# Loading v once per batch and bounding its norms with ScalarE's sums, in a hashed attention followed by an MoE block

## The chip, the cores and the metric

The kernel runs on one core of one Trainium2 chip. The metric is device time in microseconds (us), the median of several executions. Five engines run side by side, each with its own queue that is worked off in order: TensorE (PE in the profile, with its weight loads as PEld), VectorE (DVE), ScalarE (ACT), GpSimd (POOL) and SyncE (SP). SP computes nothing here and issues all DMA transfers.

## The reference, cut to what matters

```python
# batch 4, heads 8, sequence 768, head size 64; proj 64 x 6
q_bits = (einsum('bhsd,dk->bhsk', q, proj) > 0)      # the same for k
mask = q_bucket[:, :, :, None] == k_bucket[:, :, None, :]
scores = where(mask, scale * q @ k.T, -1e9)
e = exp(scores - max(scores)); attn = e / (sum(e) + 1e-9)
x = (attn @ v)  # brought to 3072 tokens x 512
h = maximum(x @ w_in, 0)                              # 512 -> 2048
out = (h * h) @ w_out                                 # 2048 -> 512
```

## The kernel before

**Precision.** The large products run in 16-bit floats, in high and low parts: a float32 value is multiplied by a power of two, rounded to f16 (the high part, `move`), and the remainder is rounded again (the low part, `left`, always one VectorE instruction when the scale is a tile). The power of two must come from a bound on the data, so each batch's v is read through once for a norm before it is split. That norm is only an upper bound: it sets an exponent.

**Tiling.** A *unit* (`unit`) is 128 query rows of one head: the scores (tile `pS`) on PE, their maximum `nmx` on DVE, `e` = exp on ACT with its row sum `sm`, the reciprocal `rv`, the high part of `hl` mostly on ACT and the low part on DVE, and a transposing DMA from `hl` to `aT`. There are 192 units. A *visit* is three units of each of two heads and ends with `av`, the product of `aT` with the split values `VV` (PE, tile `pA`, result `xx`). Eight visits make a batch. After four visits of one half of a batch, one of eight MoE stages (`moe`) follows: 16 steps `f`, each 12 matmuls into `pm`, the square on ACT, high and low parts `g`, and 9 matmuls into `po`. The weights `win` and `wo` are loaded and split while the first batch runs. At the end of the first MoE stage `align` multiplies all 16 blocks of `wo` by a power of two.

**The values.** `values(b, hp)` gives the split values of a pair of heads, [128, 2, 6, 128] f16, 3072 bytes per partition. The first call for a batch runs `scale_values`: for each of the four pairs of heads it loads v (384 KB, tile `RV`, two buffers), squares it in place, reduces the squares on DVE to 12 sums `rows` and these to one maximum `vtop`, and then forms the bound over all partitions with a small matmul (`top`, `dg`, `pt`, `norm`). Afterwards `values` loads the same 384 KB again into an `RV`, since the squares have overwritten it, and splits that into `VV` (four buffers).

**What sets the order.** The kernel records all operations first. `Program.order` is a planner: it walks the operations with a priority from their `rank` and with its own cost figures, and it chooses the engine where several may do an operation (`move`, `square`). It keeps the best of several rounds, and every engine's queue is then written out in that order (`emit`). Where the planner sees a gap on PE before the first `pm`, `emit` writes filler matmuls (`idle<-ones`) into it. So a change to one operation can move many others on all engines.

The lines to follow: `square`, `scales` and `load` are helpers within the main function; `scale_values` and `values` are called from the loop over visits with the rank `u - 6 + PREP`, plus `VALUES`.

Of the kernel before, what the change touches and what calls it, by code (L numbers as in the profile page):

```python
# [23 lines left out]
P = 128  # L24
# [3 lines left out]
KC = S // P  # L28
# [5 lines left out]
ASC = float(2.0**14)  # L34


BUFS = dict(xx=12, hl=3, raw=2, f=7, e=3, aT=3, g=2, A=2, Q=2, L=2, M=2, RV=2, VV=4)
PRICE = dict(pe=1, dve=3.57, act=0.3, pool=3.06, sp=0.43)
AHEAD, DELAY, LAG = 60, 2500, 1.0

ROUNDS, BEHIND = 4, 40000

PREP, STACKS, VALUES = -9, 0, 2
WIN_RANK, WOUT_RANK = (18, 2.0), (30, 2.5)
# [17 lines left out]
        ("act", "dve"): 100, ("act", "pool"): 180, ("pool", "dve"): 70, ("pool", "act"): 50, ("pool", "sp"): 140}  # L62


SWITCH = 95


class Buffer:
# [44 lines left out]
class Program:  # L113
# [59 lines left out]
    @staticmethod  # L173
    def cost(key, name, args, kw):

        size = lambda x: int(np.prod(x.shape[1:]))
        column = {F32: 4 / 2.4, F32R: 0.445}
        if name == "matmuls":

            side = {32: 4, 64: 2}.get(size(args[0][0][1]), 1)  # L180
            t = sum(size(a[2]) * column.get(a[2].dtype, 1 / 2.4) + 7 for a, _ in args) / side
            return t, t
        kinds = [x.rec.kind if isinstance(x, View) else "" for x in args]
        ptr = any(isinstance(x, View) and x.shape[-1] == 1 for x in args[2:3])
        n = max(size(args[0]), size(args[1]) if isinstance(args[1], View) else 0)
        if key == "pe":
            t = max(107, size(args[2]) * column.get(args[2].dtype, 1 / 2.4) + 3)
            return t, t
        if name.startswith("dma"):
            b = int(np.prod(args[0].shape)) * mybir.dt.size(args[0].dtype)  # L190
            inside = name == "dma_start_transpose" or kinds[:2] == ["sb", "sb"]
            busy = 1040 if key == "pool" else (650 if inside else 475) + 50 * (key == "act")
            return busy, b / (175 if name == "dma_start_transpose" else 314)
        if key == "act":
            t = 93 * (isinstance(kw.get("scale"), View) + isinstance(kw.get("bias"), View)) + (51 if "psum" in kinds[:2] else 93) + n / 1.2 + 93 * ("accum_out" in kw)
        elif key == "pool":
            t = 147 + n * (2.1 if args[0].dtype == F32 or args[0].dtype == F32R else 1.88) if name == "tensor_tensor" else 161 + n / 1.2 + 83 * ptr
        else:
            fast = name in ("tensor_copy", "tensor_scalar") and "psum" not in kinds[:2]
            both = len(args) > 3 and isinstance(args[3], View) and args[3].shape[-1] == 1  # L200
            t = 67 + n / (1.92 if fast else 0.96) + 62 * (ptr and (fast or name == "scalar_tensor_tensor")) + 100 * both
        return t, t

    @staticmethod
    def tiling(o):

        _, w, x = (o.args[0][0] if o.name == "matmuls" else o.args)[:3]
        size = lambda n: min(m for m in (32, 64, 128) if n <= m)
        return size(w.shape[0]), 128 if w.dtype == F32R else size(int(np.prod(w.shape[1:])))

    @staticmethod
    def port(key, name, args, kw):
# [82 lines left out]
    def forward(self, prio, near):  # L295
        ops = self.ops
        left = [len(o.deps) + len(o.after) for o in ops]
        for o in ops:
            o.queue, o.open = None, set()
        keys = ("pe", "dve", "act", "pool", "sp")  # L300
        later = {k: [] for k in keys}
        ready = {k: [] for k in keys}
        free = dict.fromkeys(keys, 0.0)
        out, dma, dge, held, kind = [], 0.0, 0.0, 0.0, None

        def offer(i):
            for w in ops[i].ways:
                k = w[0].key
                at = max([ops[j].end + LAG * LAGS.get((ops[j].queue.key, k), 200) for j in ops[i].deps] + [ops[j].start for j in ops[i].after], default=0.0)
                heapq.heappush(later[k], (at, i))  # L310
                ops[i].open.add(k)

        for i in range(len(ops)):
            if not left[i]:
                offer(i)
        while True:
            best = None
            for k in keys:
                if ready[k]:
                    t = free[k]  # L320
                elif later[k]:
                    t = max(free[k], later[k][0][0])
                else:
                    continue
                if best is None or t < best[0]:
                    best = t, k
            if best is None:
                break
            t, k = best
            while later[k] and later[k][0][0] <= t:  # L330
                i = heapq.heappop(later[k])[1]
                heapq.heappush(ready[k], (prio[i], i))
            i = heapq.heappop(ready[k])[1]
            o = ops[i]
            if o.queue is not None:
                continue
            way = next(w for w in o.ways if w[0].key == k)
            if way[5] and held > t and (ready[k] or later[k] and later[k][0][0] < held):
                heapq.heappush(later[k], (held, i))
                continue  # L340
            ends = {}
            if len(o.ways) > 1:
                for w in o.ways:
                    k2 = w[0].key
                    ahead = sum(ops[j].ways[0][4][0] / len(ops[j].open) for r, j in ready[k2] if ops[j].queue is None and r <= prio[i] + near and j != i)
                    ends[k2] = max(free[k2], t, held if w[5] else 0.0) + w[4][0] * PRICE[k2] + ahead + DELAY * w[1].startswith("dma")
            if any(e < ends[k] and k2 in o.open for k2, e in ends.items()):
                o.open.discard(k)
                continue
            o.queue, o.name, o.args, o.kw, (busy, done), port = way  # L350
            if port:
                t = max(t, held)
                held = t + busy
            if k == "pe":
                last, kind = kind, self.tiling(o)
                if last != kind:
                    busy, done = busy + SWITCH, done + SWITCH
            o.start, o.busy = t, busy
            if o.name.startswith("dma"):
                dge = max(dge, t) + busy if k != "pool" else dge  # L360
                busy = dge - t if k != "pool" else busy
                dma = max(dma, t + busy + (650 if k != "pool" else 450))
                if o.name == "dma_start_transpose":
                    o.busy = busy = dma + 467 - t
                dma += done
                done = dma + 910 - t
            free[k], o.end = t + busy, t + done
            out.append(i)
            for j in o.users:
                left[j] -= 1  # L370
                if not left[j]:
                    offer(j)
        assert len(out) == len(ops), (len(out), len(ops))
        return out
# [40 lines left out]
def lsh_attention_moe(ctx: ExitStack, tc, kq, v, proj2, w_in, w_out, consts, out):  # L415
# [27 lines left out]
    def sb(shape, dtype, name, bufs=1, tag=None):  # L443
        return pr.tile(sbp, "sb", shape, dtype, name, BUFS.get(tag or name, bufs), tag)
# [164 lines left out]
                out.append(((Q, A), (M, L)))  # L609
        return out  # L610

    vscales = {}

    def load(b, hp):
        RV = sb([P, 2, KC, D], F32, "RV")
        send(RV, v[b, hp])
        return RV

    def scale_values(b):

        tops = sb([P, H // 2], F32, "vtop", 2)
        for hp in range(H // 2):
            RV = load(b, hp)
            rows = sb([P, 2 * KC], F32, "rows", 2)
            square(RV, RV)
            dve.tensor_reduce(rows, RV.rearrange("p h c d -> p (h c) d"), AX.X, ALU.add)
            dve.tensor_reduce(tops[:, hp : hp + 1], rows, AX.X, ALU.max)
        top = sb([P, 1], F32, "top")
        dve.tensor_reduce(top, tops, AX.X, ALU.max)
        dg = sb([P, P], BF16, "dg")  # L630
        move(dg, ident, top)
        pt = ps([P, 512], F32, "pt", tag="misc")[:, 0:P]
        pe.matmul(pt, ones, dg, start=True, stop=True)
        norm = sb([P, 1], F32, "norm")
        dve.tensor_reduce(norm, pt, AX.X, ALU.max)
        vscales[b] = scales(norm, "v", 4)

    def values(b, hp):

        r0 = pr.rank  # L640
        pr.rank = r0 + VALUES
        if b not in vscales:
            scale_values(b)
        RV = load(b, hp)
        VV = sb([P, 2, KC, 2 * D], F16, "VV")
        move(VV[:, :, :, 0:D], RV, vscales[b][0])
        left(VV[:, :, :, D:], RV, vscales[b][0], VV[:, :, :, 0:D])
        return VV
# [212 lines left out]
```

## Time and profile before

| what | before |
|---|---|
| median of 3 runs | 924.09 us (924.06 to 924.19) |
| the profiled execution's own time | 925.36 us |
| its span, first to last instruction | 923.6 us |
| busy PE / DVE / ACT / POOL | 885.6 / 643.8 / 663.6 / 54.8 us |
| mean granted TensorE clock | 0.996 of full speed |
| filler matmuls | 756 (54.7 us of the busy PE) |
| moved by DMA | 149.99 MB |

The profiled execution is 1.27 us longer than the median, and 1.76 us of its time lie outside the span. The busy PE contains the filler. Almost all instructions are recorded in one helper line (402), so the rows are told apart by the tiles that they write and read: `RV<-RV` is the square, `rows<-RV` the reduction, `VV<-RV,tov` the split. The squared weights and activations have one name in the profile with their results (`g<-g`). A wait is put down to the engine that came last.

### The profile page before, as it was taken

The numbers are of one execution on the slowest core, as the hardware profiler recorded it, in microseconds if no ns is written. First come the engines' busy times: TensorE is split into PE (matmuls) and PEld (weight loads), VectorE is DVE, ScalarE is ACT, GpSimd is POOL, SyncE is SP. The second block draws the span as 40 slices with busy tenths as digits, with TensorE's granted clock in tenths as the row PEclk, the third lists the DMA queues.
The fourth block names the chain that finished last, engine by engine and source line by source line (L and its number), as shares of the span: only waits on it lengthen the run. The fifth ranks groups of instructions, "written<-read, shape, count | busy, mean of one in ns | idle before, by whom it ended". The sixth has DMA issues, their size and how long they took to land.

```text
span 923.6 us, 15264 instructions
## 1 busy us (share of the span) xinstructions
PE 885.6 (96%) x5592; PEld 501.3 (54%) x5592; DVE 643.8 (70%) x1206; ACT 663.6 (72%) x1166; POOL 54.8 (6%) x104
## 2 busy tenths in 40 slices
PE   7988988999997999999999999999999999999997
PEld 6555555445554555555555556555555555554553
DVE  5999999988979687889686768797867651211111
ACT  4877987878879677888777768787778673533433
POOL 0111301200103000000000000000000000000000
PEclk9999999999999999999999999999999999999999
DMA  7998999997999797999697959897878640200000
GB/s 236 248 222 210 226 237 213 250 211 193 236 203 242 133 192 148 185 234 244 145 198 159 190 121 198 174 213 154 170 149 177 121 102 10 77 1 0 35 1 35
DMA packets 329323, 149.99 MB, mean 162 GB/s; under 512 B 305568, under 2 KB 305696, under 8 KB 329248
## 3 DMA queue, kind: packets, MB, share of 16 engines
q1 hardware_dynamic: 329248, 149.02, 73.6%
q8 instruction: 44, 0.72, 0.3%
q14 instruction: 31, 0.25, 0.1%
HBM read 43.59 MB, written 6.29 MB: 54 GB/s over the span
## 4 chain that ended last, share of the span: by engine, by line
PE 63%; ACT 5%; DMA 2%; DVE 2%; issue 1%; POOL 0%; SPq 0%; ACTq 0%; DVEq 0%
PE po L402 23%; PE pm L402 21%; PE pS L402 9%; PE pA L399 8%; ACT wo L402 1%; DMA aT<-hl 1%; ACT e L402 1%; PE pd L399 1%; DMA RV<-vp 1%; ACT hl L402 1%; DVE hl L402 1%; ACT g L402 1%; PE pc L402 1%; DVE nmx L402 1%; DMA M<-Q 1%
## 5 line engine op out<-in xcount | busy, mean ns | idle before, releaser
L402 PE MATMUL po<-wo,g 128*128 128x512 f16 x1152 | 332.7, 381 | 2.7 <-ACT wo L402 0.9
L402 PE MATMUL pm<-xx,win 128*128 128x384 f16 x1536 | 322.4, 327 | 1.3 <-DVE g L402 1.0
L402 DVE TENSOR_REDUCE nmx<-pS 128x1 f32<-128x768 f32 x192 | 183.1, 954 | 57.7 <-PE pS L402 56.6
L402 ACT ACTIVATE e<-pS,nmx 128x768 f32<-128x768 f32 x192 | 171.6, 894 | 67.8 <-DVE nmx L402 48.8
L402 DVE SCALAR_TENSOR_TENSOR hl<-e,rv,hl 128x768 f16<-128x768 f32 x192 | 194.1, 1012 | 26.1 <-ACT hl L402 25.5
L402 PEld LDWEIGHTS <-win 128*128 128x128 f16 x1536 | 145.1, 98 | 115.4 <-issue 17.8
L402 ACT ACTIVATE hl<-e,rv 128x768 f16<-128x768 f32 x188 | 173.5, 928 | 25.1 <-ACT e L402 14.0
L402 PEld LDWEIGHTS <-g 128*128 128x128 f16 x1152 | 107.9, 98 | 131.3 <-issue 26.4
L402 DVE SCALAR_TENSOR_TENSOR g<-g,g 128x384 f16<-128x384 f32 x122 | 67.5, 554 | 127.7 <-ACT g L402 127.1
L402 ACT ACTIVATE g<-pm 128x384 f32<-128x384 f32 x125 | 60.7, 486 | 108.3 <-PE pm L402 107.4
L402 ACT ACTIVATE g<-g 128x384 f32<-128x384 f32 (+1 forms) x248 | 128.8, 520 | 10.8 <-PE po L402 5.6
L399 PE MATMUL pA<-aT,VV 128*64 128x384 f16 x1152 | 117.8, 331 | 0.0
L402 PE MATMUL pS<-A,Q 128*128 128x384 f32 x288 | 95.2, 411 | 5.0 <-ACT e L402 4.8
L399 PEld LDWEIGHTS <-VV 128*64 128x64 f16 x1152 | 59.5, 109 | 55.8 <-issue 35.8
L402 PE MATMUL pS<-L,M 128*128 128x384 f32 x288 | 77.8, 350 | 0.2
L402 PEld LDWEIGHTS pS<-A,Q 128*128 128x128 f32 x288 | 49.3, 190 | 29.8 <-ACT e L402 15.9
L402 POOL TENSOR_SCALAR rv<-sm 128x1 f32<-128x1 f32 x74 | 28.8, 389 | 610.6 <-ACT e L402 604.0
L395 PEld LDWEIGHTS <-ones 128*128 128x128 bf16 x756 | 49.9, 103 | 20.1 <-issue 11.8
L395 PE MATMUL idle<-ones 128*128 128x128 bf16 x756 | 54.7, 228 | 2.7 <-DVE ones L402 2.7
L402 PEld LDWEIGHTS pS<-L,M 128*128 128x128 f32 x288 | 51.9, 189 | 3.9 <-issue 2.4
L402 PE MATMUL pS<-Q,M 128*128 128x384 f32 x96 | 37.3, 510 | 9.5 <-ACT e L402 9.1
L402 PE MATMUL pS<-A,L 128*128 128x384 f32 x96 | 36.6, 508 | 5.7 <-ACT e L402 5.4
(92 smaller groups left out, 579.9 us busy)
## 6 DMA issues: line engine op xcount, KB each, us to landing
RV<-vp SPq DMA_DIRECT2D x32, 384.0 KB
R<-kq SPq DMA_DIRECT2D x24, 384.0 KB
raw<-w_in SPq DMA_DIRECT2D x16, 511.8 KB
raw<-w_out SPq DMA_DIRECT2D x16, 511.8 KB
out<-o SPq DMA_DIRECT2D x21, 256.0 KB
Q<-L SPq DMA_DIRECT2D x24, 192.0 KB
Q<-A SPq DMA_DIRECT2D x24, 192.0 KB
L<-M SPq DMA_DIRECT2D x24, 192.0 KB
```

What stands on the lines that cost most here:

```text
L395: issue(q, q.engine.matmul(self.idle[0].real(), self.idle[1].real(), self.idle[1].real(), start=True, stop=True).ins)
L399: ins = q.engine.matmul(*map(real, args), **kw).ins
L402: ins = getattr(q.engine, o.name)(*map(real, o.args), **{k: real(x) for k, x in o.kw.items()}).ins
```

## The change

- A batch's four pairs of heads are loaded once, by `scale_values`, into tiles that share the buffers of `VV`: six instead of four. The dictionary `loaded` hands each on to `values`, which no longer loads anything. `RV` and its two buffers are gone. Loaded and split values turn in one ring of six: the first four of a batch's places hold v as loaded, the next four the split values, and a place is taken again when all work on what stood in it is done.
- The squares no longer overwrite v. One ScalarE instruction per pair of heads squares it into a scratch tile `sqv` (bf16), which nothing reads, and adds up the whole row of 768 as it goes (`accum_out`, into a column of `tops`, called `vtop` in the profile). The two DVE reductions per pair of heads are gone. The bound is taken over a sum of 768 squares instead of the largest of 12 sums of 64; it is still an upper bound, and may give a smaller power of two.
- The squares of v are now fixed to ScalarE; `square` left the choice to the planner, which had put all 16 on ScalarE.
- `LOADS` is 0, `ENTRY` is 0, and `TRANSPOSES` has the value that stood in the code before, so these three leave the planner's rules as they were.

```diff
-BUFS = dict(xx=12, hl=3, raw=2, f=7, e=3, aT=3, g=2, A=2, Q=2, L=2, M=2, RV=2, VV=4)
+BUFS = dict(xx=12, hl=3, raw=2, f=7, e=3, aT=3, g=2, A=2, Q=2, L=2, M=2, RV=2, VV=6)
+LOADS = 0
...
-    vscales = {}
-
-    def load(b, hp):
-        RV = sb([P, 2, KC, D], F32, "RV")
-        send(RV, v[b, hp])
-        return RV
+    vscales, loaded = {}, {}
 
     def scale_values(b):
 
+        r0 = pr.rank
         tops = sb([P, H // 2], F32, "vtop", 2)
         for hp in range(H // 2):
-            RV = load(b, hp)
-            rows = sb([P, 2 * KC], F32, "rows", 2)
-            square(RV, RV)
-            dve.tensor_reduce(rows, RV.rearrange("p h c d -> p (h c) d"), AX.X, ALU.add)
-            dve.tensor_reduce(tops[:, hp : hp + 1], rows, AX.X, ALU.max)
+            pr.rank = r0 + LOADS * hp
+            RV = loaded[b, hp] = sb([P, 2, KC, D], F32, "V", tag="VV")
+            send(RV, v[b, hp])
+            act.activation(sb([P, 2, KC, D], BF16, "sqv"), RV, AF.Square, accum_out=tops[:, hp : hp + 1])
...
+        pr.rank = r0
 
     def values(b, hp):
...
         if b not in vscales:
             scale_values(b)
-        RV = load(b, hp)
+        RV = loaded.pop((b, hp))
         VV = sb([P, 2, KC, 2 * D], F16, "VV")
```

**How the instructions move.** The whole program has 16 loads of v instead of 32, 16 squares with a sum on ScalarE, and 32 reductions fewer on DVE. The planner answers with another order on every engine. Of the filler matmuls 682 are left of 756, and the first `pm` on PE stands behind 43 units instead of 44.

The first place is the start of SP's queue. `A`, `Q`, `R` are the first heads' keys and queries, `RV` or `V` is v, `sgn_f` holds signs that the first hash masks need, `raw` are weights. Before:

```order
L402 DMA A<-kq 128x768
L402 DMA Q<-kq 128x768
L402 DMA RV<-vp 128x768 x2
L402 DMA cst<-consts 128x4
L402 DMA pj<-proj 128x6 x2
L402 DMA sgn_f<-consts 6x64 x8
L402 DMA raw<-w_in 128x2047
L402 DMA R<-kq 64x768
L402 DMA RV<-vp 128x768
```

Now:

```order
L406 DMA A<-kq 128x768
L406 DMA pj<-proj 128x6 x2
L406 DMA Q<-kq 128x768
L406 DMA cst<-consts 128x4
L406 DMA sgn_f<-consts 6x64 x8
L406 DMA R<-kq 64x768
L406 DMA raw<-w_in 128x2047
L406 DMA R<-kq 64x768
L406 DMA V<-vp 128x768 x2
```

The first two loads of v have gone from ahead of the small constants to behind both `R`.

The second place is the start of DVE's queue, behind its memsets, as far as the first maxima `nmx`. `sgn` is the cast of the signs, `L` and `M` are masks, `top` and `f` prepare weights. Before:

```order
L402 TENSOR_REDUCE rows<-RV 128x12
L402 TENSOR_REDUCE vtop<-rows 128x1
L402 TENSOR_REDUCE rows<-RV 128x12
L402 CAST sgn<-sgn_f 128x512
L402 TENSOR_REDUCE vtop<-rows 128x1
L402 TENSOR_SCALAR L<-pc,cst 128x384
L402 TENSOR_SCALAR top_73<-raw 128x512
L402 TENSOR_SCALAR L<-pc,cst 128x384
L402 SCALAR_TENSOR_TENSOR f<-raw,top_73 128x512
L402 TENSOR_SCALAR M<-pc,cst 128x384 x2
L402 TENSOR_SCALAR top_77<-raw 128x512
L402 TENSOR_REDUCE rows<-RV 128x12
```

Now:

```order
L406 CAST sgn<-sgn_f 128x512
L406 TENSOR_SCALAR L<-pc,cst 128x384 x2
L406 TENSOR_SCALAR top_72<-raw 128x512
L406 SCALAR_TENSOR_TENSOR f<-raw,top_72 128x512
L406 TENSOR_SCALAR M<-pc,cst 128x384 x2
L406 TENSOR_REDUCE nmx<-pS 128x1
L406 TENSOR_SCALAR top_75<-raw 128x512
```

The reductions are gone, the two `L` stand together, and the first `nmx` is ahead of the second `top` (before, a second `f` followed the last row shown, and then the first two `nmx`).

The third place is `align` on ACT, the copies `wo<-wo,rel` between the exponentials `e`. Before:

```order
L402 ACTIVATE e,sm<-pS,nmx 128x768
L402 ACTIVATE wo<-wo,rel 128x2x512
L402 ACTIVATE A<-R,cst 128x768
L402 ACTIVATE hl<-e,rv 128x768
L402 ACTIVATE e,sm<-pS,nmx 128x768
L402 ACTIVATE wo<-wo,rel 128x2x512 x2
```

Now:

```order
L406 ACTIVATE e,sm<-pS,nmx 128x768
L406 ACTIVATE wo<-wo,rel 128x2x512
L406 ACTIVATE bits<-pd,thr 128x384
L406 ACTIVATE wo<-wo,rel 128x2x512
L406 ACTIVATE e,sm<-pS,nmx 128x768
L406 ACTIVATE wo<-wo,rel 128x2x512 x3
L406 ACTIVATE e,sm<-pS,nmx 128x768
L406 ACTIVATE wo<-wo,rel 128x2x512 x2
```

Ahead of the rows shown of before stand four groups of three such copies, each behind one `e`. ACT has 12 of the 16 copies now instead of 15, DVE three instead of one, POOL one instead of none, and they stand at the 61st to 66th unit instead of the 67th to 72nd.

More of the change, by code (lines that the diff above doesn't have):

```diff
@@ L62 @@
         ("act", "dve"): 100, ("act", "pool"): 180, ("pool", "dve"): 70, ("pool", "act"): 50, ("pool", "sp"): 140}
-SWITCH = 95
+SWITCH, ENTRY = 95, 0
+TRANSPOSES = 175
 class Buffer:
@@ L192, in cost @@
             busy = 1040 if key == "pool" else (650 if inside else 475) + 50 * (key == "act")
-            return busy, b / (175 if name == "dma_start_transpose" else 314)
+            return busy, b / (TRANSPOSES if name == "dma_start_transpose" else 314)
         if key == "act":
@@ L208, in tiling @@
         size = lambda n: min(m for m in (32, 64, 128) if n <= m)
-        return size(w.shape[0]), 128 if w.dtype == F32R else size(int(np.prod(w.shape[1:])))
+        return size(w.shape[0]), 128 if w.dtype == F32R else size(int(np.prod(w.shape[1:]))), w.dtype == F32R
     @staticmethod
@@ L355, in forward @@
                 last, kind = kind, self.tiling(o)
-                if last != kind:
+                if last is None or last[:2] != kind[:2]:
                     busy, done = busy + SWITCH, done + SWITCH
+                elif kind[2] and not last[2]:
+                    busy, done = busy + ENTRY, done + ENTRY
             o.start, o.busy = t, busy
```

## Prediction

> **What bounds the kernel now.** I read the busy times by stage first, cutting where the first `pm` starts (169.5 us), where PE becomes full (300) and where the last maximum of the attention is taken (757). Columns: stretch, its length, then busy us (and instructions) of PE, weight loads, DVE, ACT, POOL, the granted clock, the DMA share and GB/s.
>
> ```profile
> 0.00:20.00 20.00, 14.62 (x143) 12.46 (x144) 9.14 (x20) 7.68 (x10) 0.20 (x4) 0.91 0.74 220
> 20.00:170.00 150.00, 132.51 (x1087) 83.02 (x1086) 143.70 (x287) 120.77 (x202) 24.64 (x43) 1.00 1.01 228
> 170.00:300.00 130.00, 122.43 (x727) 66.82 (x725) 117.71 (x227) 112.78 (x190) 18.27 (x31) 0.99 0.97 223
> 300.00:757.00 457.00, 455.50 (x2766) 257.11 (x2765) 346.40 (x626) 355.19 (x636) 11.64 (x26) 1.00 0.83 172
> 757.00:923.60 166.60, 160.52 (x878) 81.94 (x875) 26.89 (x50) 67.17 (x132) 0.00 (x0) 1.00 0.07 22
> ```
>
> PE looks busy everywhere, but before the first `pm` much of that is filler. The same stretches for the filler tile alone, and what DVE waited for between 20 and 200 us (total, times, longest):
>
> ```profile
> 0.00:20.00 20.00, 11.81 (x125) 0.91 0.74 220
> 20.00:170.00 150.00, 42.91 (x631) 1.00 1.01 228
> DVE nmx L402 <- PE pS L402: 2.2, 6, 0.5
> ```
>
> So there are three regimes. From 0 to 20 the pipe fills. From 20 to 170 DVE sets the pace, busy 143.7 of 150 with 2.2 us of waiting for scores; PE does 132.5 - 42.9 = 89.6 us of real work there. From 300 to 757 PE is full (1.5 us idle) while DVE and ACT have a quarter of their time free; the tail is MoE on PE alone. PE's remaining work after the first `pm` is fixed, so the end moves only if the front is shorter or PE idles less after 170: 7.6 us idle until 300, 1.5 after that. DVE or ACT time saved behind 300 us is worth nothing.
>
> **What is removed and added, by price.** Groups: engine, operation, tiles, shapes and count; busy us, mean ns of one; idle time ahead and its releaser.
>
> ```profile
> L402 DVE TENSOR_REDUCE rows<-RV 128x12 f32<-128x768 f32 x16 | 15.0, 945 | 6.7 <-ACT RV L402 6.6
> L402 DVE TENSOR_REDUCE vtop<-rows 128x1 f32<-128x12 f32 x16 | 2.3, 159 | 0.1
> L402 ACT ACTIVATE RV<-RV 128x768 f32<-128x768 f32 x16 | 13.2, 834 | 6.8 <-DMA RV<-vp 6.8
> L402 ACT ACTIVATION_READ_ACCUMULATOR e<-pS,nmx 128x1 f32 x192 | 37.2, 194 | 0.0
> RV<-vp SPq DMA_DIRECT2D x32, 384.0 KB
> ```
>
> DVE loses 16 x (945 + 159) ns = 17.7 us. DMA loses 16 loads of 384 KB, 6.3 MB of 150. ACT keeps 16 squares and gets 16 reads of the accumulator, 16 x 194 ns = 3.1 us. By these counts alone one would hope for 17 us; by the stages most of it is hidden. A batch has a quarter of it, and only the first batch lies in the DVE-bound stretch, half of it even before 20 us. The reads cost nothing on ACT at 120.8 of 150 and 355 of 457 busy; without that cover one square beside `align` would cost its 0.2 us, which I leave out of the sum.
>
> **Term A, the start.** The rows of the first 25 us (start, length, engine, operation):
>
> ```profile
> 1.65 0.90 SPq L402 DMA_DIRECT2D RV<-vp  x2
> 4.04 5.31 SPq L402 DMA_DIRECT2D sgn_f<-consts  x8
> 12.86 0.43 DVE L402 CAST sgn<-sgn_f 128x512 bf16<-128x512 f32 x1 [2.89 <-DMA raw<-w_in]
> 14.72 0.46 DVE L402 TENSOR_SCALAR top<-raw 128x512 f16<-128x512 bf16 x1 [0.33 <-DMA raw<-w_in]
> 15.07 0.67 DVE L402 TENSOR_SCALAR L<-pc,cst 128x384 f32<-128x384 f32 x1
> 16.64 0.63 ACT L402 ACTIVATE sq<-f 128x512 bf16<-128x512 f32 x1
> 17.18 0.83 ACT L402 ACTIVATE L<-R 64x768 f32<-64x768 f32 x1
> 18.30 2.80 PE L402 MATMUL pS<-A,L 128*128 128x384 f32 x8
> 19.02 0.94 DVE L402 TENSOR_REDUCE rows<-RV 128x12 f32<-128x768 f32 x1
> 20.48 1.84 DVE L402 TENSOR_REDUCE nmx<-pS 128x1 f32<-128x768 f32 x2
> 22.21 0.96 DVE L402 TENSOR_REDUCE rows<-RV 128x12 f32<-128x768 f32 x1
> 23.14 0.24 DVE L402 TENSOR_REDUCE vtop<-rows 128x1 f32<-128x12 f32 x2
> 23.62 0.25 DVE L402 TENSOR_SCALAR dg<-ident,top 128x128 bf16<-128x128 bf16 x1
> ```
>
> The chain is: `sgn_f` lands, `sgn` is cast (12.86), the masks `L` follow, ACT copies `A<-L` and `L<-R`, PE makes the first scores (18.30), DVE takes the first `nmx` (20.48). In the new order two loads of v no longer stand ahead of `sgn_f` on SP: 0.90 us. At least 0.4 remains if the cast really waited for `raw`, as the row says, since `raw` now stands behind one `R`; at most it is the two transfers themselves, 786 KB at the 220 GB/s that the first 20 us move, 3.6 us. I take 1.0, near the issue row, because the DMA queue is not full there. Next, `top` no longer stands between the two `L`: 15.07 - 14.72 = 0.35. `L<-R` no longer waits behind `sq`: 17.18 - 16.64 = 0.54. The first unit's scores are done at half of the eight matmuls, 19.7, and `nmx` came at 20.48 behind `rows` and `f`; without them about 0.5 is gained. A = 1.0 + 0.35 + 0.54 + 0.5 = 2.4 us, bounds 0.4 and 3.6 + 1.4 = 5.0. The loads of v are late in turn: they stand behind both `R`, but what they feed, the first split, is needed by the first `av` only, at 49.2 us:
>
> ```profile
> L399 PE MATMUL pA<-aT,VV x1152: 326/326/350, 49.2 to 853.0; 128*64 128x384 f16 x192
> ```
>
> **Term B, the DVE-bound stretch.** Behind the first `nmx` there stood one `rows`, two `vtop` and one `dg` (which the new order has on ACT): 0.96 + 0.24 + 0.25 = 1.45 us of an engine that has no slack. B = 1.45. The lower bound is 0, if DVE's own gaps (6.3 us of the 150) grow; the upper is 2.9, since a few other rows of about 0.48 us that DVE had are elsewhere in the new order.
>
> **Term C, the first `pm`.** It now stands behind 43 units instead of 44.
>
> ```profile
> 169.50 1.30 PE L402 MATMUL pm<-xx,win 128*128 128x384 f16 x7
> ```
>
> With the first `nmx` at 20.48 and the first `pm` at 169.50 a unit takes 149 / 44 = 3.4 us. That unit's scores (half of the 2.80 us above) are paid on PE later, so the gain is at most 2.0. It is 0 if PE merely waits at that place. I take 1.0.
>
> **Term D, `align`.** The chain that ended last runs through ACT's copies just before 300 us, and there PE idles and its clock drops:
>
> ```profile
> 275.96 3.12 ACT wo L402 x3
> 295.71 2.08 ACT wo L402 x2
> L402 ACT ACTIVATE wo<-wo,rel 128x1024 f16<-128x1024 f16 x15 | 16.2, 1138 | 0.0
> 290.00:295.00 5.00, 3.80 (x22) 2.10 (x20) 4.92 (x11) 4.91 (x8) 0.81 (x1) 1.00 1.13 233
> 295.00:300.00 5.00, 3.31 (x12) 1.63 (x12) 4.71 (x10) 4.75 (x8) 0.38 (x2) 0.80 1.00 240
> 300.00:305.00 5.00, 5.00 (x23) 3.12 (x22) 3.04 (x5) 3.50 (x8) 1.58 (x2) 0.86 0.90 196
> ```
>
> PE loses 1.20 + 1.69 us of idling and 0.20 x 3.31 + 0.14 x 5.00 = 1.4 us of clock, together 4.3. The new order leaves ACT 12 of these copies instead of 15, 3.4 us less in a stretch where ACT is full. That can remove all 4.3 or nothing (ACT has squares of the third batch nearby too). I take half, D = 2.1.
>
> The other loads saved, and the 8.8 us of reductions of batches two and three, fall between 170 and 300, where PE idles 7.6 us in all, most of it counted in D. Those of the last batch fall behind 300: nothing.
>
> **Sum.** 2.4 + 1.45 + 1.0 + 2.1 = 7.0 us. The profiled execution took 925.36, so it would take 918.4; the median is 1.27 lower: **917.1 us**. The lower bounds together give 0.4 us, the upper 14.
>
> **Rivals.** *The front does not follow (14 in 100).* The reductions were in gaps that stay, or the new order merely waits elsewhere; only the issue time of A and a little of D remain, 1.5 us: 922.6. Against it: DVE's 2.2 us of waiting.
>
> *More than the sum (10 in 100).* `sgn_f` came late because of the transfers, and `align` stops hurting: 2.6 us more in A and 2.2 in D, so 912.3. For it: both are single waits which the change touches; against it: each upper bound needs its whole wait to go.
>
> *Slower: the ring of six (5 in 100).* Batch two's first split must wait for the place of batch one's third pair of heads, whose last `av` is the eighth. It stands after the 50th unit on PE, the split at the 53rd on DVE and ACT. The rate there:
>
> ```profile
> 220.00:240.00 20.00, 5.71 (x6) 5.20 (x11) 1.00 0.70 168
> ```
>
> That is six maxima in 20 us, 3.3 us each, so three units are a slack of 10 us. If the `av` is later than that, the split holds DVE and ACT, which work in order, and behind it every maximum and exponential. To use up the 7.0 and cost 2 more it must be 19 us late: 926.
>
> *Slower: the clock (6 in 100).* Where PE waited 2.5 us for the signs, the clock fell behind it:
>
> ```profile
> PE pc L402 <- DVE sgn L402: 2.5, 1, 2.5
> 12.00:16.00 4.00, 2.50 (x26) 2.23 (x27) 2.45 (x6) 0.23 (x1) 0.00 (x0) 0.83 0.99 310
> 16.00:20.00 4.00, 4.00 (x28) 3.02 (x26) 3.02 (x6) 3.90 (x6) 0.00 (x0) 0.74 1.04 294
> ```
>
> With 74 filler matmuls fewer, such gaps can come back. Real PE work until 170 is 89.6 us over some 44 units, 2.0 each; at half clock 4.1, more than the 3.4 that DVE allows, so PE would set the pace at 0.7 us a unit. To cost 9 us it must hold for 13 units: 926. Against it, the filler is written by the same rule per gap as before. The Trainium skill, TensorE: Matmul & The Clock Gate, section "What's actually happening", says that an idle window of about 3.4 us sets half clock. By that rule gaps shorter than this would do no harm; the trace has the clock lower behind 2.5 us, so it agrees in kind, and the window is not shown here.
>
> **How the numbers follow.** The sum has 65 in 100, with its own range of 913.5 to 921. A measurement of this kernel tells 0.2%, 1.85 us, from no change: 922.24. The sum and the larger gain lie wholly below it, the front that does not follow mostly inside: faster 0.79, within 0.2% 0.10, slower 0.11. The range for 8 in 10 runs from 910.5, near all upper bounds, to 923.0, which takes in the front that does not follow; the two slower cases stay outside.
>
> **What would show it.** Right: `sgn` cast about 1 us earlier and the first `nmx` near 18; the first `pm` between 162 and 166; PE idle between the first `pm` and 300 below 7 us; the stretch behind it as full as now, the tail the same length. Wrong: a first `pm` at 168 or later (B and C); PE idle or a clock below 0.9 near `align` as before (D); idle time of DVE or ACT that ends with `pA` or with a load of v (the ring); a clock below 1.00 between 20 and 170.

## The result, and the profile after

| | before | changed | ratio, 95% interval |
|---|---|---|---|
| median, first comparison (7 executions each) | 925.67 us | 921.14 us | 0.9949 [0.9926, 0.9972] |
| median, second comparison, another chip (22 and 7) | 924.20 us | 921.01 us | 0.9971 [0.9957, 0.9985] |
| span of the profiled execution | 923.6 us | 916.6 us, in the second 919.3 us | |
| first maximum `nmx` | 20.48 us | 15.42 us | |
| first `pm` | 169.50 us | 158.92 us | |
| from the first `pm` to the end of the span | 754.1 us | 757.7 us, in the second 759.9 us | |

By the ratios the change makes the kernel faster, by 4.7 us [2.6, 6.9] in the first comparison and 2.7 us [1.4, 4.0] in the second (the medians differ by 4.5 and 3.2). 7.0 were forecast against the 924.09 known then, a time of 917.1. One kernel's executions differ by more than its first three had shown: the 22 of the kernel before lie between 920.9 and 929.5 us. The first profiled execution of the changed kernel is the fastest of its seven (918.5 us), so its span flatters the change; the second (921.1) lies at the median. One execution each of two experiments below (two loads first, plan b) took 1315 and 1475 us at a granted clock of 0.63 and 0.56, and their ratios leave it out.

The stages of the changed kernel, cut as before (the second and third row together are the old 20 to 170; columns: stretch, length, busy PE, weight loads, DVE, ACT, POOL, clock, DMA share, GB/s):

```profile
0.00:20.00 20.00, 15.54 (x148) 11.82 (x148) 8.96 (x20) 9.36 (x16) 0.21 (x5) 1.00 0.76 253
20.00:160.00 140.00, 124.58 (x1004) 77.24 (x1005) 134.77 (x265) 116.86 (x197) 22.62 (x43) 1.00 1.04 222
160.00:170.00 10.00, 9.45 (x46) 4.92 (x44) 9.62 (x17) 9.77 (x20) 3.47 (x5) 1.00 0.96 213
170.00:300.00 130.00, 125.12 (x760) 69.09 (x759) 109.04 (x206) 111.05 (x194) 16.14 (x26) 1.00 0.91 194
300.00:757.00 457.00, 451.72 (x2728) 253.50 (x2727) 343.92 (x624) 354.89 (x639) 13.51 (x25) 1.00 0.87 168
757.00:916.60 159.60, 153.53 (x841) 78.29 (x838) 24.52 (x44) 63.80 (x125) 0.00 (x0) 1.00 0.08 23
```

DVE is still full until the first `pm`. PE idles 4.9 us between 170 and 300 where it idled 7.6, but 5.3 us between 300 and 757 where it idled 1.5. The tail idles 6.1 us as before. The start, and the first `pm`, in rows of the timeline (start, length):

```profile
3.08 3.60 SPq L406 DMA_DIRECT2D sgn_f<-consts  x8
8.38 0.43 DVE L406 CAST sgn<-sgn_f 128x512 bf16<-128x512 f32 x1 [5.71 <-DMA sgn_f<-consts]
13.91 2.76 PE L406 MATMUL pS<-A,L 128*128 128x384 f32 x8
15.42 0.96 DVE L406 TENSOR_REDUCE nmx<-pS 128x1 f32<-128x768 f32 x1 [0.63 <-PE pS L406]
158.92 2.11 PE L406 MATMUL pm<-xx,win 128*128 128x384 f16 x12
```

The signs are cast 4.48 us earlier (8.38 instead of 12.86), and this time the row names `sgn_f` itself as what the cast waited for. The new operations, by group (busy us, mean ns; then idle time ahead):

```profile
L406 ACT ACTIVATE sqv<-V 128x768 bf16<-128x768 f32 x16 | 13.4, 836 | 2.1 <-DMA V<-vp 2.1
L406 ACT ACTIVATION_READ_ACCUMULATOR sqv<-V 128x1 f32 x16 | 3.1, 191 | 0.0
L406 ACT ACTIVATE wo<-wo,rel 128x1024 f16<-128x1024 f16 x12 | 13.2, 1143 | 0.0
L406 DVE TENSOR_SCALAR wo<-wo,rel 128x1024 f16<-128x1024 f16 x3 | 2.2, 764 | 0.0
L406 POOL TENSOR_SCALAR wo<-wo,rel 128x1024 f16<-128x1024 f16 x1 | 1.9, 1928 | 6.4 <-PE po L406 6.4
```

The square with its sum costs what the square did (834 ns), and the read of the accumulator 191 ns, as estimated. Near `align`, in stretches of five us, PE idles 1.66 + 1.01 us and the clock stays at 1.00 (it idled 1.20 + 1.69 before, and the clock fell to 0.80 and 0.86):

```profile
265.00:270.00 5.00, 3.34 (x19) 1.87 (x19) 4.97 (x10) 5.00 (x9) 0.97 (x3) 1.00 0.98 255
270.00:275.00 5.00, 3.99 (x23) 2.54 (x23) 3.69 (x7) 5.00 (x7) 1.26 (x2) 1.00 0.78 139
```

### The profile page after: what moved, and what is told of

It reads as the page before. It is cut to its first block, busy times and chain, and to the rows that moved or that the text cites. A ratio compares the mean times of both kernels' runs of the same rounds, so it can differ in the third digit from the quotient of the medians.

```text
span 916.6 us, 15063 instructions
## 1 busy us (share of the span) xinstructions
PE 879.9 (96%) x5518; PEld 494.9 (54%) x5518; DVE 630.8 (69%) x1173; ACT 665.7 (73%) x1186; POOL 55.9 (6%) x101
## 5 line engine op out<-in xcount | busy, mean ns | idle before, releaser
L406 ACT ACTIVATE g<-g 128x384 f16<-128x384 f32 (+1 forms) x249 | 129.5, 521 | 6.6 <-PE po L406 1.6
L406 PE MATMUL pS<-L,M 128*128 128x384 f32 x288 | 75.7, 344 | 1.4 <-DMA M<-Q 1.2
L406 POOL TENSOR_SCALAR rv<-sm 128x1 f32<-128x1 f32 x71 | 31.2, 440 | 562.0 <-ACT e L406 561.9
L399 PEld LDWEIGHTS <-ones 128*128 128x128 bf16 x682 | 43.9, 101 | 22.7 <-issue 14.5
L399 PE MATMUL idle<-ones 128*128 128x128 bf16 x682 | 48.7, 225 | 2.7 <-DVE ones L406 2.7
L406 DVE TENSOR_SCALAR rv<-sm 128x1 f32<-128x1 f32 x121 | 18.3, 151 | 36.4 <-ACT e L406 33.4
```

Source lines behind the costliest of these rows:

```text
L399: issue(q, q.engine.matmul(self.idle[0].real(), self.idle[1].real(), self.idle[1].real(), start=True, stop=True).ins)
L406: ins = getattr(q.engine, o.name)(*map(real, o.args), **{k: real(x) for k, x in o.kw.items()}).ins
```

## The experiments

Two questions were open: which of the saved pieces are worth something, and how much of the result is the work and how much the order that the planner happens to write for it. So in one half of the runs a kernel's order was kept instruction by instruction and one piece was put back or moved; in the other half the planner was run anew.

### The changed kernel again

No edit; the control of the three runs after it.

> The changed kernel unaltered, as the control for the three runs beside it on the same chip. Theory (the front sets the gain: an earlier start and fewer VectorE rows until the first pm): 4 to 7 us below the kernel before, first nmx near 15.4 us, first pm near 159 us. Rival (the gain is an accident of one execution): no difference from the kernel before.

Measured: 921.01 us against 924.20, 0.9971 [0.9957, 0.9985]. The gain is real, but at 2.7 us [1.4, 4.0] it is below the 4 to 7 that were expected. Signs, first maximum and first `pm` repeat to within 0.5 us (first of the two times in each row):

```profile
L406 DVE CAST sgn<-sgn_f x1: 427/427/427, 8.2 to 8.2; 128x512 bf16<-128x512 f32 x1
L406 DVE TENSOR_REDUCE nmx<-pS x192: 932/954/960, 15.5 to 783.1; 128x1 f32<-128x768 f32 x192
L406 PE MATMUL pm<-xx,win x1536: 322/326/338, 159.4 to 909.7; 128*128 128x384 f16 x192
```

### The first two loads of v first again

```diff
+        first = [first two loads of v in the order]
+        out = [i for i in out if i not in first]
+        at = [n for n, i in enumerate(out) if self.ops[i].name == "dma_start"][3]
+        out[at + 1 : at + 1] = first      # behind A, pj, pj, Q; ahead of cst and sgn_f
```

> The changed kernel with its own order on every engine, but the first two loads of v on SP stand ahead of cst and sgn_f again. Theory (these two loads held the signs, and the start passes to the end one to one): sgn is cast 3 to 4.5 us later than the 8.4 us of the changed kernel, the first nmx moves from 15.4 to 18.5 to 20 us, and the end is 3 to 5 us later than the changed kernel's. Rival (VectorE has slack to catch up, or the signs were late for another reason): end within 1 us of the changed kernel. A cost of only the issue time would be 0.9 us.

Measured: 921.76 us, 0.9975 [0.9964, 0.9987]: 0.75 us over the control in the medians, 1.8 us in the spans of the profiled executions (921.1 and 919.3). The same rows of this run:

```profile
L410 DVE CAST sgn<-sgn_f x1: 427/427/427, 10.5 to 10.5; 128x512 bf16<-128x512 f32 x1
L410 DVE TENSOR_REDUCE nmx<-pS x192: 935/954/959, 19.0 to 784.9; 128x1 f32<-128x768 f32 x192
L410 PE MATMUL pm<-xx,win x1536: 322/326/338, 162.3 to 911.5; 128*128 128x384 f16 x192
```

The two loads do hold the signs (10.5 us against the control's 8.2) and the first maximum (19.0 against 15.5), and 2.9 us are left of it at the first `pm`. Not all of the 3.5 us at the first maximum are the signs: behind them VectorE waits 1.67 us for `raw` ahead of a mask, PE stands 2.28 us for that mask, and its clock falls to half while it makes the first scores (rows in the last section). At the end 0.75 us are left in the medians; the two intervals overlap, so it may be nothing, but they leave no room for 2.9. A later front is at least in part made up. Where, the profiles can't tell: behind the first `pm` this run took 758.8 us and the control 759.9, but two executions of the changed kernel alone differ there by 2.2 (757.7 and 759.9). One to one, which the prediction assumed, falls.

### The reductions put back

```diff
+            if o.name == "activation" and o.args[2] == AF.Square and "accum_out" in o.kw:
+                issue(self.dve, self.dve.engine.tensor_reduce(rows.real(), src, AX.X, ALU.add).ins)
+                issue(self.dve, self.dve.engine.tensor_reduce(most.real(), rows.real(), AX.X, ALU.max).ins)
```

> The changed kernel with its own order, and behind each of the 16 squares VectorE again does the two reductions (a sum over 64 for each of 12 groups of v, and a maximum over these), whose results nothing uses. That is 16 x 1.10 = 17.7 us of VectorE. Theory (only what lies before the first pm counts): 1.5 to 4 us later than the changed kernel, the 12 pairs of the later batches hidden. Rival A (VectorE time counts everywhere): 10 to 18 us later. Rival B (all hidden): within 1 us.

Measured: 929.06 us, 1.0058 [1.0041, 1.0076] of the kernel before, 8.0 us over the control: more than the theory's 1.5 to 4, less than rival A's 10 to 18. The first `pm` is 1.9 us later, though all four pairs of the first batch, 4.4 us of DVE, stand ahead of it. The reductions read v itself and not its squares, at the same size.

```profile
L406 PE MATMUL pm<-xx,win x1536: 322/326/338, 161.3 to 914.1; 128*128 128x384 f16 x192
```

PE's waits behind 160 us, of the control and then of this run (total, times, longest):

```profile
PE pS L406 <- ACT e L406: 4.9, 6, 1.3
```

```profile
PE pS L406 <- ACT e L406: 8.1, 11, 1.3
```

The profiled execution is the fastest of its six (925.55 us): its span is 4.5 us over the control's, of which 2.6 lie behind the first `pm`. By the medians it would be some 6. Four of the waits have no counterpart in the control, 1.19, 0.42, 0.76 and 0.69 us, and each ends 3.6 to 4.1 us behind the start of a reduction that was put back; the last three lie behind 300 us. The last of them, from the reduction to PE (start, length):

```profile
499.22 0.95 DVE L411 TENSOR_REDUCE rows<-V 128x12 f32<-128x768 f32 x1
500.46 0.17 DVE L406 RECIPROCAL rv<-rv 128x1 f32<-128x1 f32 x1
500.71 0.93 ACT L406 ACTIVATE hl<-e,rv 128x768 f16<-128x768 f32 x1 [0.95 <-ACT sqv L406]
502.22 0.89 ACT L406 ACTIVATE e<-pS,nmx 128x768 f32<-128x768 f32 x1
503.25 0.62 PE L406 MATMUL pS<-A,Q 128*128 128x384 f32 x2 [0.69 <-ACT e L406]
```

The reductions stand ahead of `rv` on DVE; `hl`, which needs it, stands ahead of the next exponential on ACT. The stretches that the prediction took for full on PE are full only as long as every score finds its place in `pS` free. PE works in order; 1.1 us of reductions on DVE delay what ACT works on, the exponential then releases `pS` late, and PE stands, however much `pm` work is queued behind.

### The loads put back

```diff
+            if o.name == "activation" and o.args[2] == AF.Square and "accum_out" in o.kw:
+                issue(self.sp, self.sp.engine.dma_start(o.args[1].real(), <the same v again>).ins)
```

> The changed kernel with its own order, and behind each of the 16 squares SP loads the same v a second time into the same tile, 16 x 384 KB. Theory (the transfers are hidden): within 1 us of the changed kernel. Rival (the DMA engines, at a share of 1.0 from 20 to 170 us, are a second bound): the four extra loads of the first batch take 4 x 1.8 = 7 us, so 3 to 7 us later, with waits for aT, raw or R growing before the first pm.

Measured: 925.71 us, 1.0018 [1.0000, 1.0036], 4.7 us over the control. The theory falls: the transfers are not hidden in this order. The first `pm` is 2.2 us later, less than the rival's 7 for the first batch.

```profile
L406 PE MATMUL pm<-xx,win x1536: 322/326/543, 161.6 to 918.0; 128*128 128x384 f16 x192
```

Behind 160 us PE waits longer for `M<-Q`, a transfer from tile to tile that the scores need; the control's row and then this run's (total, times, longest):

```profile
PE pS L406 <- DMA M<-Q: 0.6, 2, 0.4
```

```profile
PE pS L406 <- DMA M<-Q: 6.0, 5, 2.0
```

The first of these waits ends at 211.0 us: its transfer is issued at 206.8, right behind three second loads that SP issues from 202.5 on, where the control issues it at 203.4. (The profiled execution is the second slowest of twelve, 929.4 us, so the 6.0 may be more than the median run would show.) So the price comes by way of transfers that are needed soon and stand behind the loads. Whether the engines of the DMA or SP's queue, which waits 10.3 us in all for squares ahead of the second loads, makes it was not separated.

### All of align's copies on ScalarE

```diff
+            if q in (self.dve, self.pool) and o.name == "tensor_scalar" and tuple(o.args[0].shape) == (P, 2, DM):
+                q, o.name, o.kw, o.args = self.act, "activation", {"scale": o.args[2]}, (o.args[0], o.args[1], AF.Identity)
```

> The changed kernel with its own order, but the four copies of align that VectorE and GpSimd took stand on ScalarE at the same places in the program, 16 copies there instead of 12, 4.6 us more on ScalarE. Theory of the prediction's term D (align's stall is worth 2 us of the gain): 1 to 4 us later than the changed kernel, PE idle near 265 to 275 us grows by as much. Rival (ScalarE catches up before PE runs dry): within 0.7 us.

Measured: 924.68 us, 1.0011 [0.9996, 1.0025]; set against the control's 0.9971 that is 0.4% or 3.7 us later, by way of the kernel before, since these two ran on different chips. The stall is there: PE waits 2.37 us for an exponential behind the copies, and the clock falls to half of its speed behind it (stretches of two us):

```profile
266.44 0.76 PE L408 MATMUL pS<-A,Q 128*128 128x384 f32 x2 [2.37 <-ACT e L408]
264.00:266.00 2.00, 0.07 (x2) 0.00 (x0) 0.00 (x0) 2.00 (x3) 0.00 (x0) 1.00 1.31 185
266.00:268.00 2.00, 1.56 (x6) 1.08 (x8) 0.74 (x3) 2.00 (x4) 1.23 (x3) 0.69 0.94 264
268.00:270.00 2.00, 2.00 (x14) 1.07 (x12) 1.49 (x2) 2.00 (x4) 1.17 (x2) 0.50 0.00 0
```

So where `align` stands and who does it is worth some us, and the changed order's distribution over three engines is part of the gain.

### One part alone, planned anew

```diff
-            act.activation(sb([P, 2, KC, D], BF16, "sqv"), RV, AF.Square, accum_out=tops[:, hp : hp + 1])
+            act.activation(sqv, RV, AF.Square)
+            dve.tensor_reduce(rows, sqv.rearrange("p h c d -> p (h c) d"), AX.X, ALU.add)
+            dve.tensor_reduce(tops[:, hp : hp + 1], rows, AX.X, ALU.max)
```

> One part alone, planned anew: v is loaded once into the ring of six, squared on ScalarE into a scratch tile without the sum, and VectorE reduces the squares as before. It has 17.7 us more of VectorE work than the changed kernel, but the planner knows of it. Theory (what the planner knows of, it puts into gaps; what counts is the start and the first batch): 1 to 4 us later than the changed kernel, so 0 to 3 us below the kernel before. Rival (the price found by putting the reductions back into a fixed order, 8 us, is the price of the work itself): 8 us later than the changed kernel, 4 to 5 us above the kernel before.

Measured: 926.93 us, 1.0027 [1.0012, 1.0043]: 2.5 us above the kernel before, though it has 16 loads fewer. The other part alone, in the kernel before:

```diff
-            square(RV, RV)
-            dve.tensor_reduce(rows, RV.rearrange("p h c d -> p (h c) d"), AX.X, ALU.add)
-            dve.tensor_reduce(tops[:, hp : hp + 1], rows, AX.X, ALU.max)
+            act.activation(sb([P, 2, KC, D], BF16, "sqv"), RV, AF.Square, accum_out=tops[:, hp : hp + 1])
```

> The other part alone, planned anew: the sums of squares on ScalarE and no reductions on VectorE, but v is loaded twice through its two buffers, and the split values have four. Theory (the planner hides the 16 loads): within 1.5 us of the changed kernel, 2 to 4 us below the kernel before. Rival (the loads themselves cost the 4.7 us that putting them back into a fixed order cost): level with the kernel before or above.

Measured: 931.13 us, 1.0077 [1.0056, 1.0097]: 6.7 us above the kernel before, though it has 32 DVE instructions fewer. Both theories miss; of the rivals, the second run's, level with the kernel before or above it, has the sign right. Their first `pm`:

```profile
L406 PE MATMUL pm<-xx,win x1536: 322/326/338, 157.5 to 914.1; 128*128 128x384 f16 x192
L402 PE MATMUL pm<-xx,win x1536: 322/326/524, 161.5 to 922.1; 128*128 128x384 f16 x192
```

Both reach it 8 to 12 us earlier than the kernel before, and then need 766.2 and 770.2 us to the end of their spans (923.7 and 931.7) instead of 754.1. Nothing in the work itself explains a later end: the first run has 16 loads fewer, the second 32 instructions fewer on DVE for 3.1 us of accumulator reads on ACT. What differs besides is the order and, in the first of the two, the ring of six buffers, which was not tried alone.

### The kernel before with its loads later

```diff
+        out = rest[: spot + 1] + rv[:2] + rest[spot + 1 : later + 1] + moved + rv[2:] + rest[later + 1 :]
```

Here `rv` are the first four loads, `moved` the squares and reductions of the first two, `spot` the place behind both `R`, `later` that behind the copy `L<-R`.

> The kernel before with its own order, except that its first four loads of v on SP go behind the constants and both R, and the squares and reductions of the first two behind the first masks. All work stays. Theory (a later start of 3.5 us gives 1 to 2 us at the end, as when the loads were put first again in the changed kernel): first nmx 1.5 to 3 us earlier than 20.5, end 0.5 to 2 us below the kernel before. Rival 1 (the start passes one to one): 2 to 4 us below. Rival 2 (nothing passes): within 0.5 us.

Measured: 932.31 us, 1.0091 [1.0070, 1.0111], 7.9 us above the kernel before. The edit missed its aim. The signs come early (7.8 us), but the third square then stood on ACT ahead of a copy that the first heads' masks need, and it waited for its load; its reduction, ahead of the first maximum on DVE, waited for it:

```profile
21.35 0.84 ACT L422 ACTIVATE RV<-RV 128x768 f32<-128x768 f32 x1 [3.69 <-DMA RV<-vp]
17.70 1.39 SPq L422 DMA_DIRECT2D RV<-vp  x2
22.23 0.95 DVE L422 TENSOR_REDUCE rows<-RV 128x12 f32<-128x768 f32 x1 [2.35 <-ACT RV L422]
26.12 2.93 PE L422 MATMUL pS<-A,L 128*128 128x384 f32 x4 [8.21 <-ACT e L422]
```

The first maximum is at 23.7 instead of 20.5 and the first `pm` at 177.9 instead of 169.5. It says nothing on how an earlier start passes on. PE stood 8.21 us for the first exponential, with its granted clock at 0.50 from 24 to 28 us; how the 3.2 us at the first maximum became 8.4 at the first `pm` was not followed further.

### Two more orders of the same work

```diff
-AHEAD, DELAY, LAG = 60, 2500, 1.0
+AHEAD, DELAY, LAG = 60, 2500, 1.02     # plan a; 0.98 in plan b
```

The setting only scales the delays between engines that the planner counts with. Both kernels were run with both.

> The kernel before with the same work, but the planner counts the delays between engines 2% longer, so it writes another order (12 of align's copies on ScalarE instead of 15, 741 filler matmuls instead of 756, one load of R ahead of the first weights). Theory (another order of the same work moves the time by some us either way, since the two single parts, planned anew, came out 5.5 and 10 us above the changed kernel though each has less work than the kernel before): 2 to 8 us away from the kernel before, sign open. Rival (the order matters little): within 1.5 us of the kernel before.

> The changed kernel with the same planner setting as before_plan_a. Theory 1 (the change is worth 3 to 5 us in itself): 3 to 5 us below before_plan_a. Theory 2 (the change's own work is worth about 1 to 3 us and the rest of what was measured is the luck of one order): the difference to before_plan_a lies anywhere from -10 to +6, and differs from that of the original pair by more than 3 us.

> The kernel before with the planner's delays between engines counted 2% shorter, another order of the same work (10 of align's copies on ScalarE, 729 filler matmuls, one load of v and not two ahead of the constants). Theory (orders of the same work differ by some us): 2 to 8 us away from the kernel before. Rival: within 1.5 us.

> The changed kernel with the same planner setting as before_plan_b. Theory 1: 3 to 5 us below before_plan_b. Theory 2: anywhere from 10 below to 6 above it. In both the first nmx is near 15.5 us, as no load of v stands ahead of the constants, and with before_plan_b, which has one there, near 18.

| plan | before | changed | changed minus before |
|---|---|---|---|
| the original | 924.20 us | 921.01 us, 0.9971 [0.9957, 0.9985] | -3.2 us |
| a | 917.87 us, 0.9930 [0.9917, 0.9944] | 922.19 us, 0.9971 [0.9959, 0.9983] | +4.3 us |
| b | 930.26 us, 1.0055 [1.0038, 1.0072] | 924.67 us, 1.0000 [0.9989, 1.0010] | -5.6 us |

Ratios are to the kernel before in its original order, run beside them (924.33 us in plans a and b). The work of the kernel before takes from 917.9 to 930.3 us with the order alone, 12 us apart. The changed work takes 921.0 to 924.7. Theory 2 holds in that the difference changes its sign with the setting; its 1 to 3 us for the change's own work is not shown. The first maxima of plan b, expected near 15.5 (changed) and 18 us (before), came at 14.9 and 16.6. The fastest kernel of all is the kernel *before* in plan a, 0.7% under its own original and below the changed kernel in each of its three orders.

The first `pm` of the four (before a, changed a, before b, changed b), and with the spans what is left behind it:

```profile
L402 PE MATMUL pm<-xx,win x1536: 322/326/338, 163.2 to 906.6; 128*128 128x384 f16 x192
L406 PE MATMUL pm<-xx,win x1536: 322/326/338, 156.9 to 908.9; 128*128 128x384 f16 x192
L402 PE MATMUL pm<-xx,win x1536: 322/326/338, 163.2 to 919.0; 128*128 128x384 f16 x192
L406 PE MATMUL pm<-xx,win x1536: 322/326/338, 157.3 to 914.0; 128*128 128x384 f16 x192
```

| | first `pm` | span | behind the first `pm` |
|---|---|---|---|
| before: original, a, b | 169.5, 163.2, 163.2 | 923.6, 916.1, 928.5 | 754.1, 752.9, 765.3 |
| changed: original, again, a, b | 158.9, 159.4, 156.9, 157.3 | 916.6, 919.3, 918.6, 923.7 | 757.7, 759.9, 761.7, 766.4 |

The front is shorter in every order of the changed work, by 6 to 11 us in each pair. (The first `pm` does not stand at the same place in all: behind 44, 42 and 43 units before, and 43, 42 and 42 in the changed kernel.) What follows varies by 12 us between orders of the same work, more than the front gains, and it has been longer for the changed work in each pair.

Only part of this is idle time. Between the two extreme orders of the old work, a and b, PE idles 38.1 and 44.2 us, and its busy time without the filler is 826.3 and 833.8 us, for the same matmuls. A single matmul takes as long in both (380 and 381 ns for `po`), so in b they follow one another less closely. That is the larger part of the 12.4 us between the spans, and no count of PE's idle time shows it; what makes it was not tried.

## Why the prediction was right or wrong

The direction was right, the time lay in the range, and the size was too large: 7.0 us forecast, 4.7 and 2.7 measured in two comparisons. By its steps:

**Term A, the start (2.4 us, bounds 0.4 and 5.0).** The first maximum came 5.06 us earlier, at the upper bound. The term was mis-sized in its first piece, taken as 1.0: the signs came 4.48 us earlier. The eight issues of `sgn_f` end at 6.68 instead of 9.35 us, 0.96 because they begin earlier and 1.71 because they take 3.60 us instead of 5.31, and the cast follows the last by 1.70 instead of 3.51 us. The two loads put first again took 2.3 us of it back, so the loads cause about half; the order of `pj`, `Q` and `raw`, which also changed, was not tried alone. Behind the signs the other pieces, taken as 1.39, gave 0.58: 1.01 us were lost again between the cast and the first `L`, and 1.59 gained from there on. That most of such microseconds do not reach the end was not foreseen: with the two loads put first, of 3.5 us at the first maximum less than one arrived in the medians.

**Term B, the DVE-bound stretch (1.45 us).** From the first maximum to the first `pm` it took 143.5 us instead of 149.0; a unit's 3.4 taken off, 2.1 are left for this term, between its 1.45 and its upper bound. But the step behind it, that DVE time in this stretch passes one to one, is not borne out: with the reductions put back, 4.4 us of DVE made the first `pm` 1.9 us later. (Of the first batch's four sums, three start before 20 us and not half of them, as the prediction says; the term counts only what stood behind the first maximum.)

**Term C, the first `pm`.** It stands one unit earlier, and it came at 158.9 us, outside the 162 to 166 that were given, since A was too small. What the moved unit is worth at the end was not measured alone.

**Term D, `align` (2.1 us).** PE's idling there fell from 2.9 to 2.7 us and the clock loss of 1.4 us is gone: 1.6 us. The run with all copies on ACT shows the mechanism, and the clock's part in it. There it cost 3.7 us.

**What failed** is the step ahead of the terms: "PE's remaining work after the first `pm` is fixed, so the end moves only if the front is shorter or PE idles less after 170", and "DVE or ACT time saved behind 300 us is worth nothing". The front was 10.6 us shorter, where 162 to 166 for the first `pm` allow 3.5 to 7.5, but the span only 7.0, and 4.3 in the second profiled execution. Behind the first `pm` the changed kernel needs 3.6 us more (5.8 in the second). PE idles 3.8 us more between 300 and 757 and 2.1 less ahead of that, and its busy time is 2.0 us longer, of which 1.4 are the scores of the unit that moved there. The longest of the waits behind 300, three for exponentials (0.98 us until 368.0, 1.26 until 482.0 and 0.86 until 695.4), have none of the new squares within 30 us ahead of them, so the new squares do not make them; the order is what is left as their cause. The full look of PE in that stretch was the result of one order, not a bound: putting the reductions back costs 2.6 us behind the first `pm` in its profiled execution and some 6 by the medians, and another order of the same work up to 12. So the sum came near the result in part by luck: the front was larger than its terms, and the rest gave back what had been taken as fixed. (The 757 that the prediction gives for the last maximum is the place behind the last but one; the last is at 787.4 in the kernel before. No term hangs on it.)

**The rivals.** That the front would not follow was half true: it followed in the profile and was partly lost later. The ring of six shows no wait that matters: its loads and splits caused 2.1 us of waiting on ACT, for loads, and none in front of PE. The lower clock did not come with fewer filler matmuls: the granted clock before 20 us is 1.00 instead of 0.91, and PE no longer stands 2.5 us for the signs. What was missing is a rival of its own: that a change to this kernel makes the planner draw another order, whose time can differ by several us for reasons that have nothing to do with the change.

How much the change itself is worth, apart from the order, stays open. Three pairs give -3.2, +4.3 and -5.6 us in the medians; their mean, -1.5, is smaller than the spread of the orders.

## What to carry to other kernels

Where a planner writes the order, a change is measured together with a new order: run the old and the new work in several orders (a slightly different planner setting will do) before crediting the work, and look there first for time, since here it moved the unchanged kernel by 12 us. A piece's price in a given order is found by putting it back into that order and nothing else; planned anew the same piece can differ either way (8 us against 5 for the reductions here, 4 to 5 against 10 for the loads), so the two must not be mixed. An engine that looks full in the profile but works in order on what others release is not a bound, and time saved on its suppliers still counts.

## What the runs showed of the hardware

The clock gate, which lowers PE's clock after a pause, answers to a shorter gap than expected. PE stood for 2.37 us in the run with all copies on ACT, and the granted clock was 0.69 in the two us that follow and 0.50 in the next two, 0.96 after that. A gap of 2.28 us in the run with two loads first did the same, 0.83 and then 0.50:

```profile
16.59 0.32 PE L410 MATMUL pc<-bits,sgn 128*128 128x384 bf16 x1 [2.28 <-DVE M L410]
18.00:20.00 2.00, 2.00 (x4) 1.01 (x3) 1.03 (x2) 1.48 (x4) 0.00 (x0) 0.50 1.05 408
```

The Trainium skill, TensorE: Matmul & The Clock Gate, section "What's actually happening", has half clock after an idle window of about 3.4 us; the half is what this run shows, but one gap of 2.37 us was enough here. The 2.5 us that the prediction took to agree with that rule in kind already spoke against its window.

Small loads suffer from large ones issued just ahead of them, already at their issue: eight issues of 1.5 KB took 5.31 us behind two loads of 384 KB and 3.60 us without them. In the changed kernel's fixed order, with only these two loads moved, it is 5.25 against the control's 3.58.
